# Pairing the stages of a linear-attention kernel across two batches, with paired loads and a new order

## The chip, the cores and the metric

The kernel runs on one core of a Trainium2 chip. A core has a matrix engine (TensorE, PE in the profile), a vector engine (VectorE, DVE), a scalar engine (ScalarE, ACT), a general engine (GpSimd, POOL) and a queue engine (SyncE, SP). Each runs its own instructions in order and waits on semaphores for the others. Sixteen DMA engines move data; DMAs are issued by SyncE, ScalarE and GpSimd, and in this kernel those from GpSimd convert float32 to bfloat16 on the way. The metric is the device time of one execution in microseconds (us).

## The reference

A recurrence with a decaying state per batch and head (4 batches, 8 heads, 768 steps, 48 features), followed by a two-layer network over all 3072 tokens (384 to 2048 to 384 features) with a leaky ReLU:

```python
for t in range(S):
    kt, vt, rt = k[:, :, t], v[:, :, t], r[:, :, t]
    cur = np.einsum('bhd,bhe->bhde', u[None] * kt, vt)
    y[:, :, t] = np.einsum('bhd,bhde->bhe', rt, state + cur)
    state = w[None, :, :, None] * state + np.einsum('bhd,bhe->bhde', kt, vt)
x = y.transpose(0, 2, 1, 3).reshape(B * S, H * D)
h = x @ w_in
g = np.maximum(0.01 * h, h)
out = g @ w_out
```

## The kernel before

**Stages.** The 768 steps of a batch are cut into 6 chunks of 128; a stage is one chunk of one batch, so there are 24. In the kernel before, stage n is chunk n % 6 of batch n // 6: all chunks of a batch come one after the other, and the state goes from stage n to stage n + 1, except at a batch's start.

**One stage.** Its steps have one letter each, followed by the stage's number:
- `k`, `r`, `v` load the stage's data with GpSimd (`load_one`, DMA on L284), 128 rows of 8 heads of 48 features. Stage 0 is loaded by SyncE and ScalarE instead (`load_early`, `v0` and the cast `U0`). Rings: 10 places for r and k side by side (`rk_sb`), 10 for v.
- `P` (`scaled`, L399) multiplies r and k by powers of the decay on VectorE. The result is transposed: stages 0 to 7 by TensorE (`T`, L421, with the ScalarE eviction `C`, L432), the rest by a DMA transpose that SyncE issues (`X`, L410).
- `A` (L481) forms the 128 x 128 scores of all 8 heads on TensorE, `M` masks them on VectorE: for stages 0 to 5 by a product (L491, L502, or `m` and `N`), for the others by a predicated copy (L505) into a tile whose diagonal is there already. That diagonal comes from `E`, `f`, `R` (VectorE, L442, L447, L452: u times k, times r, summed) and `L` (GpSimd, L467, which fills the tile). Stages 0 to 5 have `D` and `V` (VectorE) in their place.
- `K` (L539) is the product of keys and values on TensorE. `B` (`state_sum`, L570 or L573) adds the old state and `W` (`state_mul`, L578) decays the sum. Stages in `CARRY` add the old state on TensorE.
- `Y` (L609) adds scores times values and queries times state into PSUM; `O` (L627) evicts that to `xT` on ScalarE.

**The network.** It works on pairs m of stages 2m and 2m + 1. `J` (`up_two`, L664, 6 matmuls of 256 columns) is an eighth of the first layer, `j` (L673) its eviction with the leaky ReLU; stages 0 and 1 have some narrow ones (`G`, L642, 12 matmuls of 128 columns). The second layer is done in seven half-size products in place of eight (`Z`, L766, 8 matmuls of 192 columns each), with sums of `g` and of the weights on VectorE beforehand (`b`, L735; `t`, L716) and evictions `z` on ScalarE (L777, L782) and VectorE (L787). `o` stores a stage's 128 rows. `i` and `w` load the weights (L296, L300), `p` is the set-up of tables, masks and constants, `q` clears padding.

**Fills.** `F1.256.10@0` is one TensorE matmul on constants (L387) whose result nobody reads. There are 21, before and between the first transposes.

**The order.** `ORDER` is one list of steps, written out. `Sched.add` takes them in that order, and works out which semaphores each must wait for; each engine then plays its own steps in just that order. `@5` is the PSUM bank of a step (`@01` two of them); a step that writes a bank waits until the one before has been read. So a step that waits holds back all later steps of its engine, whatever they need.

## Time and profile before

| | |
|---|---|
| median of 3 runs | 164.97 us (164.47 to 165.57) |
| profiled execution | 165.07 us |
| its span, first to last instruction | 163.3 us |
| VectorE busy | 130.5 us, 260 instructions |
| ScalarE busy | 88.2 us, 194 instructions |
| GpSimd busy | 88.1 us, 101 instructions |
| data moved by DMA | 19.89 MB in 100234 packets |

The busy times are those of one profiled execution. A GpSimd DMA row shows the time in which GpSimd writes the transfer's descriptors; when its data have landed stands in rows of their own. Matmuls overlap each other, so the time of one is longer than the distance to the next. "L284" is a line of the kernel, "x23" a count, and a bracket behind a row of the time-ordered list tells how long the engine had been idle and what ended that.

### The profile page before, as it was taken

What the parts mean: (1) busy time and instruction counts of PE and PEld (TensorE: products, weight loads), DVE (VectorE), ACT (ScalarE), POOL (GpSimd) and SP (SyncE); (2) the same over time, 40 slices, a digit from 0 to 9 for tenths busy, and PEclk for the clock granted to TensorE, in tenths of its full rate; (3) what the DMA queues carried; (4) which work ended last, traced back from release to release, by engine and by line L of the source; (5) the groups of instructions that cost most, each with busy time, mean ns of one, the idle gap of its engine ahead of it and who ended that gap; (6) DMA issues with size and microseconds to landing.
All of it is one profiled execution on the core that took longest, in us unless ns stands there. A gap on an engine that the chain in (4) does not pass through costs nothing.

```text
span 163.3 us, 5367 instructions
## 1 busy us (share of the span) xinstructions
PE 154.8 (95%) x2299; PEld 137.6 (84%) x2299; DVE 130.5 (80%) x260; ACT 88.2 (54%) x194; POOL 88.1 (54%) x101
## 2 busy tenths in 40 slices
...
GB/s 105 137 167 167 154 174 163 186 204 144 145 121 161 100 151 152 130 145 87 150 131 211 264 128 151 230 4 0 62 199 52 0 4 0 0 18 180 4 98 193
DMA packets 100234, 19.89 MB, mean 122 GB/s; under 512 B 93169, under 2 KB 100210, under 8 KB 100210
## 3 DMA queue, kind: packets, MB, share of 16 engines
...
q10 hardware_dynamic: 1328, 0.39, 1.0%
...
## 4 chain that ended last, share of the span: by engine, by line
PE 60%; POOL 21%; DVE 9%; DMA 6%; issue 2%; POOLq 0%; DVEq 0%
PE ps_all L766 28%; PE ps_all L664 25%; POOL rk_sb L284 11%; DMA rk_sb<-in_r_dram 6%; POOL v_sb L284 4%; PE ps_all L609 3%; PE ps_all L481 2%; POOL w_out_sb L300 2%; POOL w_in_sb L296 2%; DVE qk L399 2%; DVE at L505 2%; POOL at L467 1%; PE ps_all L539 1%; DVE out_sb L787 1%; DVE s_tok L452 1%
## 5 line engine op out<-in xcount | busy, mean ns | idle before, releaser
L673 ACT ACTIVATE gT<-ps_all 128x512 bf16<-128x512 f32 x92 | 52.0, 604 | 29.3 <-PE ps_all L766 14.1
L664 PE MATMUL ps_all<-xT,w_in_sb 128*128 128x256 bf16 x552 | 66.6, 273 | 0.5 <-DVE at L505 0.5
L664 PEld LDWEIGHTS ps_all<-xT,w_in_sb 128*128 128x128 bf16 x552 | 52.4, 98 | 7.3 <-DVE at L505 0.8
L467 POOL TENSOR_SCALAR_AFFINE_SELECT at<-s_tok 128x1024 bf16<-128x1024 f32 x18 | 20.6, 1155 | 27.0 <-DVE s_tok L452 26.9
L766 PE MATMUL ps_all<-tw,gs 128*128 128x192 bf16 x288 | 28.3, 246 | 0.1
L735 DVE TENSOR_TENSOR gs<-gT 128x1024 bf16<-128x1024 bf16 x24 | 16.1, 686 | 11.1 <-ACT gT L673 5.8
L284 POOL DMA_DIRECT2D rk_sb<-in_k_dram x23 | 21.0, 918 | 7.2 <-DVE ku L442 6.4
L766 PEld LDWEIGHTS ps_all<-tw,gs 128*128 128x128 bf16 x288 | 24.0, 98 | 0.4 <-issue 0.3
L505 DVE CAST_PREDICATED at<-mask,ps_all 128x1024 bf16<-128x1024 uint16 x18 | 21.5, 1216 | 2.0 <-PE ps_all L481 1.8
L284 POOL DMA_DIRECT2D v_sb<-in_v_dram x23 | 21.1, 923 | 0.6 <-PE ps_all L539 0.6
L284 POOL DMA_DIRECT2D rk_sb<-in_r_dram x23 | 21.3, 932 | 0.0
L766 PE MATMUL ps_all<-w_out_sb,gT 128*128 128x192 bf16 x192 | 19.8, 246 | 0.0
L787 DVE TENSOR_TENSOR out_sb<-ps_all,snap 128x192 f32<-128x192 f32 x37 | 12.6, 351 | 5.9 <-PE ps_all L766 5.8
L627 ACT ACTIVATE xT<-ps_all 128x384 bf16<-128x384 f32 x24 | 11.0, 494 | 11.5 <-PE ps_all L609 10.3
L777 ACT ACTIVATE snap<-ps_all 128x192 f32<-128x192 f32 x36 | 11.1, 338 | 11.3 <-PE ps_all L766 10.3
L766 PEld LDWEIGHTS ps_all<-w_out_sb,gT 128*128 128x128 bf16 x192 | 16.1, 98 | 0.5
L399 DVE TENSOR_TENSOR qk<-rk_sb,tab 128x768 bf16<-128x768 bf16 x23 | 13.9, 611 | 2.9 <-DMA rk_sb<-in_r_dram 2.7
L609 PE MATMUL ps_all<-at,v_sb 128*32 128x128 bf16 x384 | 10.4, 220 | 1.1 <-DVE vs L560 1.1
L432 ACT ACTIVATE tp<-ps_all 128x512 bf16<-128x512 f32 x16 | 9.0, 596 | 3.9 <-PE ps_all L421 3.6
L609 PEld LDWEIGHTS ps_all<-at,v_sb 128*32 128x32 bf16 x384 | 8.0, 96 | 3.1 <-DVE vs L560 1.4
L766 PE MATMUL ps_all<-w_out_sb,gs 128*128 128x192 bf16 x96 | 9.9, 246 | 0.0
L782 ACT ACTIVATE out_sb<-ps_all 128x192 f32<-128x192 f32 x11 | 3.7, 332 | 11.3 <-PE ps_all L766 11.3
...
## 6 DMA issues: line engine op xcount, KB each, us to landing
...
w_out_sb<-in_moe_w_out_dram POOLq DMA_DIRECT2D x4, 384.0 KB, 11.1
tp<-qk SPq DMA_TRANSPOSE x16, 5.2
...
```

Of the source, the lines that this page charges most:

```text
L284: add("pool", lambda: G.dma_start(dst, src), W=[key], dma=f"{which}{n}")
L399: add("dve", lambda: V.tensor_tensor(qk[iq][:, :, 0:D], both, by, ALU.mult), R=[("r", n % NRK), ("k", n % NRK), "qtab", "ktab", ("qk0", iq ...
L467: add("pool", lambda: G.affine_select(out=at[ia][:, :, :, :].rearrange("p two m i -> p (two m) i"), in_=s_tok[i2][:, :].unsqueeze(2).to_br ...
L505: add("dve", lambda: V.copy_predicated(dst, mask[:, :].bitcast(mybir.dt.uint16).unsqueeze(1).to_broadcast([128, H, 128]), raw), R=keys + [ ...
L609: last = PE.matmul(ps_y[32 * q:32 * q + 32, 128 * s:128 * s + 128], a, m, start=first_mm and (s == 0 or whole), stop=last_mm and whole)
L627: add("act", lambda: A.activation(xT[m % NX][:, :, 128 * half:128 * half + 128], ps[i][:, 0:HD].rearrange("p (s t) -> p s t", t=128), AF.C ...
L664: last = PE.matmul(ps[i][:, 256 * f:256 * f + 256], w_in_sb[:, s, 128 * fb:128 * fb + 128], xT[ix][:, s, :], start=s == 0, stop=s == NSL - 1)
L673: add("act", lambda: A.activation(gT[ig][:, 2 * j:2 * j + 2, :].rearrange("p f t -> p (f t)"), ps[i][:, :], AF.Prelu, alpha=0.01), R=[key] ...
L735: add(eng, lambda: on.tensor_tensor(x[i][:, :, :], a, b, op), R=keys, W=[("gs", m % 2, i)])
L766: done = PE.matmul(ps[i][:, 0:NH], lhs[:, s, :], rhs[:, s, :], start=bool(opens) and s == 0, stop=s == HF - 1, skip_group_check=not (opens ...
L777: add("act", lambda: A.activation(snap[i2][j][:, :], ps[i][:, 0:NH], AF.Copy), R=[key], W=[("snap", i2, j)])
L787: add("dve", lambda: V.tensor_tensor(out_sb[io][:, cols], ps[i][:, 0:NH], snap[i2][j][:, :], ALU.add), R=[key, ("snap", i2, j), *after], W ...
```

## The change

- Stage n is now chunk n // 2 % 6 of batch n // 12 * 2 + n % 2. Stages 2m and 2m + 1 are the same chunk of two batches, and the state goes from stage n to stage n + 2. `CARRY` has stages 2 and 3 in place of 1 and 2 (and 0, which had no effect).
- From stage 2 on, `k`, `r` and `v` load both stages of a pair with one DMA each (`PAIRED`); the places of `rk_sb` are laid out so that the two stages lie side by side. `scaled` reads r and k of one stage from two stretches. v has 12 places in place of 10.
- Rows of the output are stored where the new numbering puts them.
- `ORDER` is new throughout and has no fills. GpSimd's list begins with the ramp, r1, k1, r2, k2, i0, v1, i1, v2, k4, r4, k6, r6; VectorE's, after the tables, with P0, P1, D0, P3, P2, M0. `INTER` is not used by the functions.

```diff
--- before.py
+++ after.py
@@ -22,57 +22,55 @@
 NSL = HD // 128
 
 VHW = {0}
-RINGS = (6, 8, 6, 6, 6, 3, 3, 8, 10, 10)
+RINGS = (6, 8, 6, 6, 6, 3, 3, 8, 10, 12)
 DIAG = {0, 1, 2, 3, 4, 5}
 SUMS_PE = set()
 KU_POOL = set()
 ST_POOL = set()
 GS_POOL = set()
-CARRY = {0, 1, 2}
+CARRY = {2, 3}
+INTER = 1
+PAIRED = {2, 4, 6, 8, 10, 12, 14, 16, 18, 20, 22}
 FIRST = {0}
 ORDER = """
-p3 p0 q1 k1 p10 p2 p8 p11 p4 F1.256.10@0 F1.256.2@1 k2 p5 p21@7 p6 p9 r1 p7 p15 p17 p13 p16 F1.512.18@6 v0 r2
-F1.128.8@5 p22 F1.256.1@6 q0 p14 p19 F1.128.28@0 p18 F1.128.18@1 q3 F1.256.9@2 q5 p23 F1.256.15@3 q4 i1 q2
-F1.256.12@4 p24 F1.128.24@5 F1.256.6@6 F1.256.0@7 r3 p31 P0.0 F1.512.1@0 P0.1 F1.256.17@1 T0.0@0 k3 F1.128.25@7
-F1.256.8@6 C0.0 F1.512.15@7 v1 P1 F1.128.9@1 T0.1@2 F1.512.8@3 P2 C0.1 T1.1@4 k5 p32 p27 U0 D0 A0@01 r5 p28
-T2.1@5 M0.1 T2.0@6 p30 F1.256.16@7 C2.1 T1.0@3 M0.0 K0@2 v2 p29 C1.0 V0 i0 C1.1 B0 Y0@7 C2.0 v3 A1@01 P3 A2@23
-m1.1 D1 r4 T3.1@4 O0 N1.1 T3.0@1 K1@5 M1.0 C3.0 k4 G0.1@6 V1 C3.1 B1 k7 Y1@7 D2 P5 r7 A3@01 O1 K2@4 D3 M3.0
-T5.1@5 i3 T5.0@7 V2 C5.0 G1.1@0 v4 M2 C5.1 G1.0@7 g1.1 k6 B2 g0.1 K3@5 G0.0@0 r6 V3 M3.1 Y2@6 g0.0 i2 P4 g1.0
-Y3@4 v7 O2 T4.1@7 O3 p1 A5@01 T4.0@6 M5.0 J1.0@2 v5 C4.0 P7 J1.2@0 C4.1 v6 D5 j1.0 B3 J1.1@6 m5.1 D4 w0 T7.0@7
...
-Z10.2 b11.2 Z10.3@7 z10.2 z11.0 Z11.1@0 z10.3 z9.4 Z10.4 Z9.5 z10.4 Z9.6 Z11.2@1 z9.6 z11.1 o19 Z11.3 z11.2 z9.5
-Z10.5 b11.3 o18 z11.3 Z11.4 z10.5 Z10.6 z11.4 z11.7 o23.0 Z11.5 z10.6 o20 o23.1 Z11.6@0 o21 z11.5 o22.1 z11.6
-o22.0
+p3 p0 p9 q1 p2 p14 p17 p8 r1 q2 p11 q0 p4 p18 p16 p5 k1 p10 p21@0 p6 p13 p15 r2 p7 v0 p22 k2 p24 p23 i0 P0.0
+P0.1 v1 T0.0@7 T0.1@6 P1 C0.0 i1 q3 T1.1@5 p19 p27 p31 p28 p32 p30 v2 p29 C0.1 C1.1 k4 D0 A0@67 U0 T1.0@0 K0@1
+r4 C1.0 P3 A1@23 P2 k6 T3.1@0 M0.0 T2.1@4 M0.1 T2.0@5 r6 V0 T3.0@6 C2.0 q4 Y0@7 D1 i3 m1.1 C2.1 N1.1 v4 B0 O0
+A2@34 M1.0 K1@5 C3.1 v6 C3.0 M2 G0.1@7 i2 V1 A3@01 p1 D3 Y1@6 B1 k8 D2 O1 q5 K2@2 M3.1 K3@3 w0 V2 G1.1@1 M3.0 w1
+Y2@4 w3 G1.0@0 P5 O2 w2 V3 T5.0@5 g1.0 T5.1@6 P4 r8 Y3@4 C5.0 B2 C5.1 G0.0@0 k10 O3 A5@56 g1.1 T4.1@2 T4.0@4 r12
+C4.1 P7 J1.0@1 M5.0 C4.0 J1.3@2 r10 m5.1 B3 T7.1@4 j1.3 D5 A4@56 P6 J1.1@3 g0.1 M4 T6.0@2 j1.1 J1.2@7 g0.0 N5.1
+T6.1@3 J0.6@5 D4 C6.0 b0.2 C6.1 K5@6 J1.7@0 C7.1 V5 K4@2 j1.0 B5 T7.0@3 V4 Y5@4 C7.0 Y4@6 O5 E6 J0.7@1 E7 O4 B4
+j1.7 J1.5@3 f7 j0.7 f6 J0.4@4 E9 j1.5 R7 A7@01 j0.4 W4 A6@23 L7 R6 J1.6@6 j1.2 W5 j0.6 J2.5@4 L6 M7 J0.5@7 k12
+J2.0@5 E8 j0.5 M6 J2.7@0 j1.6 k16 J1.4@1 j2.7 b0.0 K6@7 v12 j1.4 b1.2 Y7@6 Y6@0 b0.1 O7 J2.6@3 v8 O6 b1.0 J2.2@6
+j2.6 J3.3@2 j2.5 t0 J2.4@3 t2 J3.2@4 j2.4 J2.1@1 B6 f9 Z0.0@0 t1 Z1.0@3 j3.2 P8 Z0.1@7 j3.3 E10 f8 j2.0 K7@4 t3
+J2.3@2 z0.0 z1.0 j2.1 J3.7@5 W6 P9 j2.3 Z0.2 B7 X9 P11 J3.1@1 b1.1 Z1.1@2 j3.1 X8 P10 J3.0@4 z0.2 P12 j2.2
+Z0.3@1 b0.3 j3.0 P13 Z0.4 z0.1 z1.1 f10 X12 Z0.5 R9 W7 Z1.2 L9 E13 z0.4 Z1.3@6 R8 z1.2 E12 L8 J3.5@4 X10 z0.3
+z1.3 Z0.6 z0.5 b2.0 r14 J3.6@1 j3.5 f13 b1.3 X11 Z1.4 j3.7 r16 j3.6 A9@45 z1.4 A8@67 k18 Z2.0@1 M8 X13 Z1.5 k14
+M9 Z1.6 J3.4@6 k22 b2.1 Y8@7 R13 Y9@4 O8 b3.2 Z2.1@5 O9 b2.3 j3.4 K8@7 J4.4@4 z0.6 E11 z2.1 z1.5 z1.6 K9@6 R10
+J4.6@0 z2.0 f12 L10 J4.0@2 b3.0 j4.6 B8 J4.5@3 j4.0 B9 J4.7@0 r18 j4.5 f11 b3.1 J4.1@2 j4.4 R11 j4.7 A10@34 R12
+A11@67 j4.1 L11 Z2.2 M10 J4.3@0 v10 P17 J4.2@2 j4.3 M11 L12 Z2.3@3 j4.2 Z3.0@4 z2.2 v16 P16 P15 A12@67 z3.0
+Z3.1@0 M12 L13 Z3.2 z3.1 v14 b2.2 Z3.3@2 z3.2 E17 A13@67 z2.3 k20 b3.3 Z2.4 M13 K12@3 Z3.4 r20 Z2.5 z2.4 W9 v20
+Z3.5 B12 P18 Z4.0@6 v18 z3.4 Z2.6 W8 z3.5 b4.0 Y11@7 z2.6 Y10@3 P14 O11 Y12@0 f17 O10 X18 Y13@1 E16 Z3.6 O12 E15
+O13 K13@7 J5.7@3 X14 P19 J6.6@0 E14 j5.7 b4.2 J5.4@1 R17 J5.6@3 z2.5 j5.4 L17 f15 o0 J5.5@5 X16 j5.6 J6.4@1 z3.6
+b4.1 j5.5 J6.7@3 R15 j6.4 f16 J5.0@4 L15 X15 z3.3 j6.7 f14 J5.1@5 j6.6 E19 J6.5@1 R14 o1 J6.2@0 f19 j6.5 L14 X17
+B13 J6.0@2 b4.3 j6.2 r22 J6.3@3 j5.0 E18 j6.0 o4 J6.1@7 R19 X19 j6.3 f18 Z4.1@4 L19 j6.1 R18 z4.0 A15@01 A14@23
+L18 M15 J5.3@7 o7 Z4.2 j5.3 M14 Z4.3@0 z4.1 j5.1 K14@1 z4.2 J5.2@7 b6.0 E21 Z4.4 j5.2 B14 P20 Y14@5 Y15@7 z4.3
...
+z10.1 j11.7 J11.5@2 j11.6 Z11.0@1 j11.5 Z11.1@7 z10.0 b11.0 z9.6 Z10.2 z11.1 b11.1 z11.0 Z11.2@2 z9.5 z10.2
+b10.2 o18 Z10.3@5 o19 z11.2 o13 Z11.3 b11.3 Z11.4 z11.3 Z10.4 z11.4 z11.7 Z10.5 z10.4 o23.1 z10.3 Z10.6 z8.6
+z10.5 o17 Z11.5 z10.6 o21 Z11.6@0 z11.5 o23.0 o22.1 o20 z11.6 o22.0
 """
 
 
@@ -184,8 +182,8 @@
     HF, NH = NFB // 2, HD // 2
     w_in_sb = SB("w_in_sb", [128, NSL, DFF])
     w_out_sb = SB("w_out_sb", [128, NFB, HD])
-    rk_sb = SB("rk_sb", [128, NRK, 2, HD])
-    r_sb, k_sb = rk_sb[:, :, 0, :], rk_sb[:, :, 1, :]
+    rk_sb = SB("rk_sb", [128, NRK // 2, 2, 2, HD])
+    r_sb, k_sb = rk_sb[:, :, 0, :, :], rk_sb[:, :, 1, :, :]
     v_sb = SB("v_sb", [128, NV, H * E])
     w_row = SB("w_row", [1, HD], FP32)
     one_row = SB("one_row", [1, 128], FP32)
@@ -238,14 +236,24 @@
     def hd(x):
         return x.rearrange("p (h d) -> p h d", d=D)
 
+    def chunk(n):
+        return n // 2 % NC
+
+    def batch(n):
+        return n // (2 * NC) * 2 + n % 2
+
+    def rows_of(n):
+        at = S * batch(n) + L * chunk(n)
+        return slice(at, at + L)
+
     def early(which, n):
         return out_sb[4 + 2 * n + (which == "k")][:, :]
 
     def k_of(n):
-        return early("k", n) if n in FIRST else k_sb[:, n % NRK, :]
+        return early("k", n) if n in FIRST else k_sb[:, n % NRK // 2, n % 2, :]
 
     def r_of(n):
-        return early("r", n) if n in FIRST else r_sb[:, n % NRK, :]
+        return early("r", n) if n in FIRST else r_sb[:, n % NRK // 2, n % 2, :]
 
     def key_of(which, n):
         if n in FIRST:
@@ -263,25 +271,25 @@
 
 
     def load_early(which, n, eng):
-        src = {"k": k, "r": r}[which][0].rearrange("h t d -> t h d")[L * n:L * n + L, :, :]
+        src = {"k": k, "r": r}[which][batch(n)].rearrange("h t d -> t h d")[L * chunk(n):L * chunk(n) + L, :, :]
         dst, queue = early(which, n), {"act": A, "sp": SP}[eng]
         add(eng, lambda: queue.dma_start(dst.rearrange("p (h d) -> p h d", d=D), src),
             W=key_of(which, n), dma=f"{which}{n}")
 
     def load_one(which, n):
-        b, c = divmod(n, NC)
-        t0 = c * L
-        src = {"k": k, "r": r, "v": v}[which][b].rearrange("h t d -> t h d")[t0:t0 + L, :, :]
+        m, slots = (2 if n in PAIRED else 1), (NV if which == "v" else NRK)
+        i = n % slots
+        src = {"k": k, "r": r, "v": v}[which][batch(n):batch(n) + m].rearrange("b h t d -> t (b h) d")
+        src = src[L * chunk(n):L * chunk(n) + L, :, :]
         if which == "v":
-            dst = v_sb[:, n % NV, :].rearrange("p (h e) -> p h e", e=E)[:, :, 0:D]
+            dst = v_sb[:, i:i + m, :].rearrange("p b (h e) -> p (b h) e", e=E)[:, :, 0:D]
         else:
-            dst = {"k": k_sb, "r": r_sb}[which][:, n % NRK, :].rearrange("p (h d) -> p h d", d=D)
-        key = (which, n % (NV if which == "v" else NRK))
+            dst = {"k": k_sb, "r": r_sb}[which][:, i // 2, n % 2:n % 2 + m, :].rearrange("p b (h d) -> p (b h) d", d=D)
         if which == "v" and n in VHW:
             io = 6 + n
             add("sp", lambda: SP.dma_start(hd(out_sb[io][:, :]), src), W=[("o", io, 0), ("o", io, 1)], dma=f"v{n}")
         else:
-            add("pool", lambda: G.dma_start(dst, src), W=[key], dma=f"{which}{n}")
+            add("pool", lambda: G.dma_start(dst, src), W=[(which, i + j) for j in range(m)], dma=f"{which}{n}")
 
     def v_cast(n):
         io = 6 + n
@@ -394,9 +402,10 @@
     def scaled(n, half=None):
         iq = n % NQK
         if half is None:
-            both = rk_sb[:, n % NRK, :, :].rearrange("p w (h d) -> p (w h) d", d=D)
-            by = tab[:, :, :].rearrange("p w (h d) -> p (w h) d", d=D)
-            add("dve", lambda: V.tensor_tensor(qk[iq][:, :, 0:D], both, by, ALU.mult),
+            both = rk_sb[:, n % NRK // 2, :, n % 2, :].rearrange("p w (h d) -> p w h d", d=D)
+            by = tab[:, :, :].rearrange("p w (h d) -> p w h d", d=D)
+            to = qk[iq][:, :, 0:D].rearrange("p (w h) d -> p w h d", w=2)
+            add("dve", lambda: V.tensor_tensor(to, both, by, ALU.mult),
                 R=[("r", n % NRK), ("k", n % NRK), "qtab", "ktab", ("qk0", iq)], W=[("qp", iq), ("kp", iq)])
         elif half:
             add("dve", lambda: V.tensor_tensor(qk[iq][:, H:2 * H, 0:D], hd(k_of(n)), hd(ktab[:, :]), ALU.mult),
@@ -519,10 +528,10 @@
             R=["mask", ("at", ia, half)], W=[("at", ia, half)])
 
     def is_live(n):
-        return n % NC < NC - 1
+        return chunk(n) < NC - 1
 
     def is_carried(n):
-        return n in CARRY and n % NC > 0
+        return n in CARRY and chunk(n) > 0
 
     def keys_values(n):
         iq = n % NQK
@@ -566,17 +575,17 @@
         i, key = banks[("K", n)]
         kv = ps[i][:, 0:HD].rearrange("p (m e) -> p m e", e=2 * D)
         lock = [("kvlock", n)] if n in SUMS_PE else []
-        if n % NC == 0 or is_carried(n):
-            add("dve", lambda: V.tensor_tensor(st[(n + 1) % NT][:, :, :], kv, wl[:, :, :], ALU.mult),
-                R=[key, "wl0", "wl1"] + lock, W=[("st", (n + 1) % NT)])
+        if chunk(n) == 0 or is_carried(n):
+            add("dve", lambda: V.tensor_tensor(st[(n + 2) % NT][:, :, :], kv, wl[:, :, :], ALU.mult),
+                R=[key, "wl0", "wl1"] + lock, W=[("st", (n + 2) % NT)])
         else:
             add("dve", lambda: V.tensor_tensor(sum_t[n % 4][:, :, :], kv, st[n % NT][:, :, :], ALU.add),
                 R=[key, ("st", n % NT)] + lock, W=[("sum", n % 4)])
 
     def state_mul(n):
         eng, on = ("pool", G) if n in ST_POOL else ("dve", V)
-        add(eng, lambda: on.tensor_tensor(st[(n + 1) % NT][:, :, :], sum_t[n % 4][:, :, :], wl[:, :, :], ALU.mult),
-            R=[("sum", n % 4), "wl0", "wl1"], W=[("st", (n + 1) % NT)])
+        add(eng, lambda: on.tensor_tensor(st[(n + 2) % NT][:, :, :], sum_t[n % 4][:, :, :], wl[:, :, :], ALU.mult),
+            R=[("sum", n % 4), "wl0", "wl1"], W=[("st", (n + 2) % NT)])
 
     def outputs(n):
         it, ia, iv, is_ = n % NTP, n % NAT, n % NVS, n % NT
@@ -595,7 +604,7 @@
                 if kk > 0:
                     c1 = c0 + 16 + 32 * kk
                     one.append((v_sb[:, n % NV, c1:c1 + 32], at[ia][:, 1, p, :]))
-                if n % NC:
+                if chunk(n):
                     one.append((st[is_][:, p, 32 * kk:32 * kk + 32], tp[it][:, p, :]))
                 todo += [(s, a, m, i == 0, i == len(one) - 1) for i, (a, m) in enumerate(one)]
             return todo
@@ -617,7 +626,7 @@
         reads = [("v", n % NV), "v0", ("at", ia, 0), ("at", ia, 1), "ident", ("tp", it, 0)]
         if not whole:
             reads.append(("vs", iv))
-        if n % NC:
+        if chunk(n):
             reads.append(("st", is_))
         add("pe", emit, R=reads, W=[key])
 
@@ -696,12 +705,12 @@
     def stored(n, c=None):
         io = n % NO
         if c is None:
-            add("sp", lambda: SP.dma_start(out[128 * n:128 * n + 128, :], out_sb[io][:, :]),
+            add("sp", lambda: SP.dma_start(out[rows_of(n), :], out_sb[io][:, :]),
                 R=[("o", io, 0), ("o", io, 1)], W=[("out", n, 0)], dma=f"o{io}")
         else:
             cols = slice(NH * c, NH * c + NH)
             eng, queue = ("sp", SP) if c == 0 else ("act", A)
-            add(eng, lambda: queue.dma_start(out[128 * n:128 * n + 128, cols], out_sb[io][:, cols]),
+            add(eng, lambda: queue.dma_start(out[rows_of(n), cols], out_sb[io][:, cols]),
                 R=[("o", io, c)], W=[("out", n, c)], dma=f"o{io}{c}")
 
     def w_sum(i):
```

44 lines of the change are left out of this document (13 added, 31 removed).

## The prediction

> **What bounds the kernel now.** I read the busy shares first, then the chain in order of time, then the time-ordered list of TensorE with its idle notes.
>
> ```profile
> PE 154.8 (95%) x2299; PEld 137.6 (84%) x2299; DVE 130.5 (80%) x260; ACT 88.2 (54%) x194; POOL 88.1 (54%) x101
> ...
> 34.25 1.72 POOL rk_sb L284 x2
> 35.97 9.89 DMA rk_sb<-in_r_dram
> ...
> 62.62 2.14 PE ps_all L664 x18
> ...
> 148.75 11.89 PE ps_all L766 x144
> 160.64 0.02 issue
> 160.66 0.36 DVE out_sb L787
> ```
>
> The chain says GpSimd until 36 us, one r load until 45.9, VectorE until 62.6, then TensorE without a hole to 160.64. The first part misleads if read as "TensorE waits for loads until 62 us": a chain shows what ended last, not what TensorE did meanwhile. Its own list does (an idle time stands in brackets at a row's end):
>
> ```profile
> 16.85 0.33 PE L539 MATMUL ps_all<-v_sb,qk 128*128 128x96 bf16 x4
> ...
> 21.11 0.24 PE L609 MATMUL ps_all<-at,v_sb 128*32 128x128 bf16 x4
> ...
> 22.67 2.13 PE L664 MATMUL ps_all<-xT,w_in_sb 128*128 128x256 bf16 x18
> 24.64 0.39 PE L421 MATMUL ps_all<-ident,qk 128*128 128x128 bf16 x4
> ...
> 56.07 0.40 PE L481 MATMUL ps_all<-tp 48*128 48x128 bf16 x8 [1.39 <-DVE sum_t L573]
> ...
> 62.62 1.59 PE L664 MATMUL ps_all<-xT,w_in_sb 128*128 128x256 bf16 x13 [0.55 <-DVE at L505]
> ```
>
> From 16.85 us on it idles twice, 1.39 and 0.55 us, 1.94 in all. So the end is set by (a) when dense TensorE work starts, for which I take 22.67 us, the first wide up-projection J1.0; (b) the matmuls after it; (c) 1.94 us of stalls; (d) the tail behind 160.64. Only (a) and (c) can be won.
>
> What makes the 1.39 us stall stands in the list of all engines:
>
> ```profile
> 52.88 1.21 DVE L399 TENSOR_TENSOR qk<-rk_sb,tab 128x768 bf16<-128x768 bf16 x1
> ...
> 54.01 1.53 DVE L447 TENSOR_TENSOR ku<-rk_sb,ku 128x384 bf16<-128x384 bf16 x1
> 54.21 1.11 POOL L467 TENSOR_SCALAR_AFFINE_SELECT at<-s_tok 128x1024 bf16<-128x1024 f32 x1
> ...
> 55.94 0.34 DVE L787 TENSOR_TENSOR out_sb<-ps_all,snap 128x192 f32<-128x192 f32 x1
> 56.18 1.11 POOL L467 TENSOR_SCALAR_AFFINE_SELECT at<-s_tok 128x1024 bf16<-128x1024 f32 x1
> 56.20 2.34 DVE L505 CAST_PREDICATED at<-mask,ps_all 128x1024 bf16<-128x1024 uint16 x2
> ...
> L399 DVE TENSOR_TENSOR qk<-rk_sb,tab x23: 542/551/1209, 8.8 to 109.6; 128x768 bf16<-128x768 bf16 x23
> ...
> L447 DVE TENSOR_TENSOR ku<-rk_sb,ku x18: 345/351/1533, 30.9 to 112.3; 128x384 bf16<-128x384 bf16 x18
> ```
>
> Two VectorE products that take 0.55 and 0.35 us in the middle of their groups took 1.21 and 1.53 beside a GpSimd diagonal fill: 1.84 us lost. The eviction z1.3 (55.94) came after them, and the scores A8 of 56.07 write the bank that it empties.
>
> **The change, part by part.** The 21 fills go; the matmuls of the computation are the same in number (as many stages without a state, as many live ones, two carried ones as before). So (b) stays, and (d) too: the last steps are again z11.6 and o22.0 on the same queues.
>
> *Fewer, larger loads.*
>
> ```profile
> L284 POOL DMA_DIRECT2D v_sb<-in_v_dram x23 | 21.1, 923 | 0.6 <-PE ps_all L539 0.6
> L284 POOL DMA_DIRECT2D rk_sb<-in_k_dram x23 | 21.0, 918 | 7.2 <-DVE ku L442 6.4 <-POOLq L855 0.8
> L296 POOL DMA_DIRECT2D w_in_sb<-in_moe_w_in_dram x4 | 3.1, 786 | 0.0
> ```
>
> 69 issues become 36: three single ones and 33 pairs. A single is 128 rows times 8 heads, 1024 pieces, in 0.92 us; a w_in load is 128 times 3, 384 pieces, in 0.79. A pair, 2048 pieces, costs between 0.92 (pieces free) and 1.84 (twice a single); the line through the two rows gives 0.92 + 1024 x 0.13/640 = 1.13, which I take. GpSimd is then relieved of 66 x 0.92 - 33 x 1.13 = 23 us. None of it is TensorE time by itself: what counts is when data land, and those pieces are as many and as small as before.
>
> ```profile
> 1.31 1.93 POOL L284 DMA_DIRECT2D rk_sb<-in_k_dram  x2 [0.80 <-POOLq L855]
> ...
> 26.72 1.00 POOL L284 DMA_DIRECT2D rk_sb<-in_k_dram  x1
> ...
> 38.57 0.92 POOL L284 DMA_DIRECT2D rk_sb<-in_k_dram  x1
> DMA to landing us min/median/max: 4.4/4.4/4.4
> ...
> DMA to landing us min/median/max: 12.8/12.9/12.9
> ...
> DMA to landing us min/median/max: 9.9/10.9/11.3
> ```
>
> The three landing rows are for loads issued in 0 to 3, 24 to 28 and 36 to 40 us. The load of 26.72 landed about 39.6, that of 38.57 (twelfth, counting both) near 49.2: 9.6 us for 11 loads, 0.87 us each, with a backlog standing. That is the pace at which the DMA engines serve loads, hardly quicker than GpSimd issued singles. So pairing makes a load land no earlier, and the earlier member of a pair later.
>
> In the new order GpSimd does the ramp, r1, k1, then the pairs of r2 and k2. If r1 lands 4.4 us after an issue near 1.6, at 6.0, the k2 pair lands five loads later, 6.0 + 5 x 0.87 = 10.4; r4, twelve loads and two w_in loads (I allow 1.8 us each) behind r1, near 20.0.
>
> *The start on VectorE.* It runs in order, and the scaling of stages 3 and 2 (P3, P2) now stands ahead of the masking M0 of stage 0.
>
> ```profile
> 8.77 0.56 DVE L399 TENSOR_TENSOR qk<-rk_sb,tab 128x768 bf16<-128x768 bf16 x1 [2.15 <-DMA rk_sb<-in_r_dram]
> ...
> 10.61 1.28 DVE L491 TENSOR_TENSOR at<-ps_all,mask 128x512 bf16<-128x512 f32 x2
> ...
> 27.00 0.42 DVE L518 TENSOR_TENSOR at<-at,mask 128x512 bf16<-128x512 bf16 x1
> 27.34 0.55 DVE L560 TENSOR_TENSOR vs<-v_sb,ps_all 128x384 bf16<-128x384 bf16 x1
> 27.80 0.35 DVE L578 TENSOR_TENSOR st<-sum_t,wl 128x384 bf16<-128x384 bf16 x1
> ...
> 49.18 0.47 DVE qk L399
> ```
>
> From start to start an instruction takes 0.47 (P, V and B), 0.34 (D, N), 0.60 (half a mask) and 1.13 (a whole one, from the pair at 56.20). Up to what lets Y3 start, both orders hold the same VectorE work except B2, moved behind: 6 P, 4 V, 2 B = 5.6; 4 D, 1 N = 1.7; 5 half masks = 3.0; 1.1; small ones 0.6: 12.0 us. The tables are ready near 5.6, as now.
> - Waits before: 2.15 us for stage 1 at 8.77, and some tenths; Y3 ran at 21.11.
> - Waits after: stage 1 lands near 7, 0.5 us; D0 waits for the eviction C0.1, now behind four small ScalarE steps, 1.0 us; P3 for the k2 pair, from 9.3 to 10.4, 1.1 us; P5 for r4, about 0.5 us. Sum 3.1.
>
> V3 ends at 5.6 + 12.0 + 3.1 = 20.7 and Y3 starts there, 0.4 us earlier than before. Between Y3 and J1.0 there were 1.56 us (21.11 to 22.67); one narrow up-projection (G0.0) more is now there, 12 matmuls of 128 columns. The 18 of 256 columns at 22.67 took 1.97 us to the next row, 0.109 each, so 12 of half the width take 0.66. J1.0: 20.7 + 1.56 + 0.66 = 22.9, and with slower first transposes I take 23.1: **+0.4 us**. Shorter state chains (stage 1 no longer waits for stage 0, nor 3 for 2) don't show here, because VectorE's sum is the bound.
>
> *The middle.* By the same counting the masks of stages 8 and 9 have 0.5 us more VectorE work ahead than before, and the loads of 10 to 13 land as VectorE comes to them. But its products now meet the diagonal fills otherwise: of the four behind R9 and R8, in the order W7, E13, E12, f13, one starts with the fill and is held about 1 us, where two lost 1.84. I let the stalls fall from 1.94 to 0.6: **-1.3 us**. If E12 is held too, 1 us of it comes back.
>
> *Smaller edits.* The scaling reads its operand in two stretches of 384 instead of one of 768. Its output was already in stretches of 48, so I take nothing; if it lost its rate (768 results in 0.47 us; the mask's 1024 take 1.13), each would cost 0.85, 0.38 more, 5 us over the 13 ahead of stage 9. Twelve v places lengthen one memset by about 0.1 us, hidden by the wait for the tables. The rows of the output go elsewhere with the same pieces: nothing.
>
> *The fills.* They ran while TensorE had nothing else, so their time is free. What they may do for the matmuls after them shows in the first transposes:
>
> ```profile
> 6.52 0.63 PE L421 MATMUL ps_all<-ident,qk 128*128 128x128 bf16 x4
> ...
> 9.39 0.40 PE L421 MATMUL ps_all<-ident,qk 128*128 128x128 bf16 x4 [0.79 <-DVE qk L399]
> ...
> 0.00:10.00 10.00, 7.55 (x42) 4.25 (x42) 4.78 (x20) 5.01 (x10) 8.82 (x15) 1.00 1.36 134
> ```
>
> Four transposes took 0.63 us, later 0.40, though the granted clock reads 1.00 throughout: the first ones are slow. I put 0.2 us above for that.
>
> **Sum.** +0.4 - 1.3 = -0.9 us on the profiled execution (165.07: span 163.3 and 1.8 around it), 164.2. The median of the three runs, 164.97, lies 0.1 below it: **164.1 us**.
>
> **The rivals.**
> - *Loads land sooner* (0.27). GpSimd issues a pair at 0.57 us per load; if the engines follow at 0.7, k2 lands at 9.5, P3 waits 0.2 instead of 1.1, P5 not at all, and VectorE never waits in the middle: start -1.0, both stalls gone, -1.9. Time 164.97 - 2.9 = 162.1. For it: nothing shows what the engines do when issued faster. Against: 0.87 with a backlog. The Trainium skill, page "DMA: Bandwidth & Descriptors", section "Measured (HBM→SBUF, 128 partitions, SWDGE, issued from GpSimd)", gives about 0.67 us as the floor, that of 64 packets at 10.5 ns. A single load here puts 1024/16 = 64 pieces on each of 16 engines, so by that page k2 would land at 9.4 and this rival holds.
> - *Late pairs hold VectorE* (0.24), the one that ends slower. P3, P5, P7, the table t0 and P11, P12 each stand in order in front of masks and evictions, and each now waits for a whole pair. If a load takes 1.0 us, r4 lands 1.6 us later, and k12, some 30 loads behind r1, over 3 us later. VectorE passes it to TensorE: +2.2 over the median, 167.2. It decides from about 0.95 us per load. For it: between 40 and 48 us loads share the engines with transposes. Against: 0.87.
> - *TensorE stays slow without fills* (0.07). From T0 to J1.0 there are 12 groups of 4 transposes and 4 narrow projections of 12, at 0.055 each 5.3 us; scores, outputs and key-value groups I put at as much. If those 10.6 us all run at half speed, J1.0 comes near 6.5 + 21.2 = 27.7: +5, 170. Against it, matmuls at half speed fill the time better. The Trainium skill, page "TensorE: Matmul & The Clock Gate", section "Part 1: The HAM clock gate (the "warmup" mystery)", says that full speed comes after about 3.4 us of sustained work; the row agrees that the first are slow, and whether scattered work counts no run here shows.
> - *Nothing moves* (0.08). The state was not on the path, GpSimd's time neither; the same stalls at other places: 165.0.
>
> **How the numbers follow.** The forecast keeps 0.34, with its own range 162.9 to 165.9. One per cent, 1.65 us, is about what tells from no change here: faster means under 163.3, slower above 166.6. Faster: the first rival but for a few hundredths, and the forecast's lower edge, 0.30. Slower: second and third rival, 0.27. Within: 0.43. The range runs from 161.2 to 167.9, past the middles of the first two rivals, and leaves out the half-speed case and a lost scaling rate.
>
> **What would show it.** Pair issues near 1.13 us and landings at 0.87 per load; P3 idle for r or k until about 10.4; J1.0 near 23; one or two TensorE idles between 50 and 63 with under 1 us; then TensorE unbroken to the end. Wrong it would be by J1.0 outside 22 to 24, by a scaling over 0.6 us in the median, by holes in TensorE after 65 us, or by transposes still at 0.6 us beyond 12 us.

## The result, and the profile after

The changed kernel takes 169.54 us (median of 4 runs, 169.06 to 170.40), the kernel before on the same chip 165.27 (164.47 to 166.23): a ratio of 1.026, 95% interval 1.020 to 1.032. The change makes it slower by 4.3 us; 164.1 was forecast. (A ratio leaves out the executions over 1.5% above their kernel's fastest, medians and ranges hold all of them.) The profiled execution took 169.49 us, its span 167.4, which is 4.1 more than before.

Where the 4.1 us are shows in a table by stretches of the span: busy time of TensorE, with the number of its matmuls in brackets, weight loads, VectorE, ScalarE, GpSimd, granted clock, DMA share, GB/s. Before:

```profile
0.00:30.00 30.00, 26.26 (x414) 19.59 (x415) 22.39 (x57) 19.83 (x40) 28.82 (x39) 1.00 1.84 153
30.00:60.00 30.00, 28.61 (x442) 25.73 (x440) 28.01 (x52) 17.30 (x39) 21.54 (x24) 1.00 2.02 150
90.00:100.00 10.00, 10.00 (x164) 9.15 (x162) 9.82 (x21) 5.53 (x13) 4.15 (x5) 1.00 1.10 197
150.00:163.30 13.30, 10.63 (x129) 10.40 (x127) 5.63 (x15) 2.43 (x8) 0.00 (x0) 1.00 0.27 91
```

After:

```profile
0.00:30.00 30.00, 23.69 (x334) 18.06 (x335) 21.16 (x52) 17.67 (x36) 25.85 (x31) 1.00 1.91 155
30.00:60.00 30.00, 30.00 (x471) 27.14 (x472) 28.02 (x56) 17.57 (x37) 15.29 (x13) 1.00 1.91 161
90.00:100.00 10.00, 8.97 (x158) 8.06 (x156) 9.47 (x18) 5.38 (x11) 0.15 (x1) 1.00 1.00 153
150.00:167.40 17.40, 12.86 (x150) 12.27 (x147) 7.57 (x19) 4.82 (x13) 0.00 (x0) 0.99 0.36 125
```

By 30 us 334 matmuls are done where before it was 393 (414 less 21 fills): a late start. From 30 to 60 us TensorE has no hole, where before 1.39 us were open. From 90 to 100 us 1.03 us are new, and behind 150 us it idles 4.54 where it was 2.67.

Busy time hides slow matmuls, so I also kept a ledger: TensorE's steps in order, each with its steady start-to-start time (J and Z 0.66 us, A 0.28, T 0.22, Y about 0.5). They add up to 145.9 us in both kernels; what is lost up to a time is that time less the steps begun by then.

| TensorE's loss, us | before | after | difference |
|---|---|---|---|
| up to 30 us | 12.15 | 14.51 | +2.4 |
| 30 to 90 us | 2.40 | 0.68 | -1.7 |
| 90 to 150 us | 0.02 | 1.44 | +1.4 |
| 150 us to the last step Z11.6 | 0.00 | 1.72 | +1.7 |
| behind its start | 2.83 | 3.17 | +0.3 |

The start, VectorE's list (a bracket is idle time and what ended it):

```profile
9.07 0.43 DVE L445 TENSOR_TENSOR prod<-tp 128x512 bf16<-128x512 bf16 x1 [1.30 <-ACT tp L441]
10.50 1.03 DVE L408 TENSOR_TENSOR qk<-rk_sb,tab 128x768 bf16<-128x768 bf16 x2 [1.00 <-DMA rk_sb<-in_k_dram]
11.44 1.28 DVE L500 TENSOR_TENSOR at<-ps_all,mask 128x512 bf16<-128x512 f32 x2
...
20.41 0.55 DVE L408 TENSOR_TENSOR qk<-rk_sb,tab 128x768 bf16<-128x768 bf16 x1
20.88 0.55 DVE L569 TENSOR_TENSOR vs<-v_sb,ps_all 128x384 bf16<-128x384 bf16 x1
```

Second row: P3 and P2 wait for the k2 pair until 10.50, and the masks M0.0 and M0.1 (third row) stand behind them. Last row: V3, started at 20.88. TensorE's list, narrow up-projections of 12 equal matmuls:

```profile
15.55 1.48 PE L651 MATMUL ps_all<-xT,w_in_sb 128*128 128x128 bf16 x12
...
19.84 1.06 PE L651 MATMUL ps_all<-xT,w_in_sb 128*128 128x128 bf16 x12
...
21.52 0.83 PE L651 MATMUL ps_all<-xT,w_in_sb 128*128 128x128 bf16 x12
```

The same work takes 1.48, 1.06 and 0.83 us: TensorE is slow until about 20 us. The granted clock's column reads 1.00 there, but that is no reading: the trace's first record of the clock starts at 20.31 us (8.21 in the kernel before), and the column counts the time ahead of it as full speed. J1.0 starts at 24.97 (before: 22.67).

The later holes stand in the chain that ended last, and in TensorE's list:

```profile
88.16 0.55 SPq L708
88.71 0.04 issue
88.75 6.20 DMA tp<-qk
94.95 0.05 issue
95.00 0.40 PE ps_all L490 x8
...
158.00 3.81 DMA out_dram<-out_sb
161.81 0.02 issue
161.84 0.37 DVE out_sb L796
162.21 0.05 issue
162.25 2.17 PE ps_all L775 x24
```

```profile
95.00 0.40 PE L490 MATMUL ps_all<-tp 48*128 48x128 bf16 x8 [1.02 <-DMA tp<-qk]
...
162.25 0.83 PE L775 MATMUL ps_all<-tw,gT 128*128 128x192 bf16 x8 [1.54 <-DVE out_sb L796]
```

The scores A19 waited for the DMA transpose X19, issued at 88.75 and landed at 94.95. Z10.6 waited for a VectorE eviction of stage 21, and that for the store o13, issued at 158.00: stages 13 and 21 share place 5 of the output ring, and o13 stands behind o19 on SyncE.

### The profile page after: what moved, and what is told of

Its sections match the earlier page's. It is cut to its first block, busy times and chain, and to the rows that moved or that the text cites. A ratio compares the mean times of both kernels' runs of the same rounds, so it can differ in the third digit from the quotient of the medians.

```text
span 167.4 us, 5268 instructions
## 1 busy us (share of the span) xinstructions
PE 155.1 (93%) x2278; PEld 138.2 (83%) x2278; DVE 128.2 (77%) x260; ACT 89.0 (53%) x194; POOL 68.9 (41%) x68
## 4 chain that ended last, share of the span: by engine, by line
PE 75%; DVE 9%; DMA 7%; ACT 5%; issue 2%; SPq 1%; DVEq 0%; ACTq 0%
PE ps_all L673 28%; PE ps_all L775 27%; PE ps_all L618 5%; PE ps_all L490 5%; DMA tp<-qk 4%; PE ps_all L430 3%; DMA out_dram<-out_sb 2%; PE ps_all L548 2%; DVE gs L744 2%; PE ps_all L651 2%; DVE ku L456 2%; ACT tp L441 2%; DVE at L514 1%; DVE out_sb L796 1%; DVE s_tok L461 1%
## 5 line engine op out<-in xcount | busy, mean ns | idle before, releaser
L673 PE MATMUL ps_all<-xT,w_in_sb 128*128 128x256 bf16 x552 | 67.4, 273 | 0.3 <-DVE at L514 0.3
L476 POOL TENSOR_SCALAR_AFFINE_SELECT at<-s_tok 128x1024 bf16<-128x1024 f32 x18 | 21.4, 1198 | 51.7 <-DVE s_tok L461 48.0
L636 ACT ACTIVATE xT<-ps_all 128x384 bf16<-128x384 f32 x24 | 10.9, 492 | 16.4 <-PE ps_all L618 10.4
L775 PE MATMUL ps_all<-w_out_sb,gT 128*128 128x192 bf16 x192 | 19.1, 246 | 0.0
L292 POOL DMA_DIRECT2D v_sb<-in_v_dram x12 | 13.8, 1158 | 2.3 <-issue 2.3
L408 DVE TENSOR_TENSOR qk<-rk_sb,tab 128x768 bf16<-128x768 bf16 x23 | 13.1, 579 | 2.1 <-DMA rk_sb<-in_k_dram 1.0
L292 POOL DMA_DIRECT2D rk_sb<-in_r_dram x12 | 14.0, 1167 | 1.3 <-PE ps_all L430 1.0
L292 POOL DMA_DIRECT2D rk_sb<-in_k_dram x12 | 13.7, 1145 | 0.0
L490 PE MATMUL ps_all<-tp 48*128 48x128 bf16 x192 | 9.2, 232 | 2.9 <-ACT tp L441 1.7
L775 PE MATMUL ps_all<-tw,gT 128*128 128x192 bf16 x96 | 9.9, 246 | 1.5 <-DVE out_sb L796 1.5
L490 PEld LDWEIGHTS ps_all<-tp 48*128 48x128 bf16 x192 | 5.9, 99 | 5.8 <-ACT tp L441 2.5
```

The lines of the kernel that those rows point to most:

```text
L292: add("pool", lambda: G.dma_start(dst, src), W=[(which, i + j) for j in range(m)], dma=f"{which}{n}")
L408: add("dve", lambda: V.tensor_tensor(to, both, by, ALU.mult), R=[("r", n % NRK), ("k", n % NRK), "qtab", "ktab", ("qk0", iq)], W=[("qp", i ...
L476: add("pool", lambda: G.affine_select(out=at[ia][:, :, :, :].rearrange("p two m i -> p (two m) i"), in_=s_tok[i2][:, :].unsqueeze(2).to_br ...
L490: last = PE.matmul(ps[i][:, 128 * p:128 * p + 128], tp[it][at_rows, NP + p, :], tp[it][at_rows, p, :], start=True, stop=True)
L673: last = PE.matmul(ps[i][:, 256 * f:256 * f + 256], w_in_sb[:, s, 128 * fb:128 * fb + 128], xT[ix][:, s, :], start=s == 0, stop=s == NSL - 1)
L775: done = PE.matmul(ps[i][:, 0:NH], lhs[:, s, :], rhs[:, s, :], start=bool(opens) and s == 0, stop=s == HF - 1, skip_group_check=not (opens ...
```

## The experiments

All are the changed kernel with the edit shown, but for e2, which is the kernel before. "Loss" is that of the ledger; the kernel before on the same chips took 165.0 to 165.7 us.

| run | median, us | ratio to before (95%) | J1.0 at | loss to 30 us | loss from there to Z11.6 |
|---|---|---|---|---|---|
| before | 165.27 | 1 | 22.67 | 12.15 | 2.42 |
| changed | 169.54 | 1.026 (1.020 to 1.032) | 24.97 | 14.51 | 3.84 |
| e1_fills | 169.73 | 1.022 (1.018 to 1.026) | 24.13 | 13.77 | 3.80 |
| e2_before_nofills | 166.70 | 1.006 (1.004 to 1.009) | 24.05 | 13.54 | 2.20 |
| e3_o13 | 169.40 | 1.023 (1.019 to 1.028) | 24.18 | 13.82 | 3.72 |
| e4_x19 | 169.54 | 1.024 (1.019 to 1.029) | 24.21 | 13.85 | 3.96 |
| e5_o13 | 168.31 | 1.022 (1.014 to 1.030) | 24.29 | 13.93 | 5.06 |
| e6_singles | 172.29 | 1.043 (1.037 to 1.049) | 24.80 | 14.34 | 7.34 |
| e7_start | 172.32 | 1.040 (1.033 to 1.047) | 22.78 | 15.32 | 4.52 |
| e8_all | 168.09 | 1.017 (1.012 to 1.022) | 22.87 | 15.41 | 0.96 |
| e9_three | 166.52 | 1.008 (1.005 to 1.012) | 25.09 | not read | not read |
| e10_start | 168.53 | 1.020 (1.014 to 1.025) | 24.63 | 16.32 | 1.36 |
| e11_i1 | 172.85 | 1.048 (1.042 to 1.054) | 28.05 | 19.27 | 2.27 |
| e12_i0 | 167.30 | 1.009 (1.005 to 1.013) | 24.60 | 14.15 | 2.18 |
| e13_start | 166.24 | 1.000 (0.997 to 1.004) | 22.90 | 12.62 | not read |
| e14_r22 | 167.51 | 1.012 (1.008 to 1.017) | 22.73 | 12.71 | not read |
| e15_r14 | 168.50 | 1.017 (1.012 to 1.022) | 22.91 | 12.62 | 3.22 |

("Not read" stands where the profiled execution was one of the kernel's longest; the other figures of e9, e13 and e14, and those of e5, come from such an execution too.)

**The fills.** 16 of before's fills put back (and `p10`, the memset of their operand, moved forward); and, in e2, the 21 taken from the kernel before.

```diff
-... p21@0 p6 ... T1.1@5 p19
+... F1.256.10@1 F1.256.2@2 p21@0 F1.512.18@3 ... F1.256.0@1 p6 ... T1.1@5 F1.512.1@2 F1.512.15@3 F1.512.8@4 p19
```

> The changed kernel with 16 of the constant matmuls back: two before the matmul of the decay row, eleven behind it, three behind the first transposes of stage 1; the memset of their operand is moved forward. Theory (TensorE runs at half speed until 20.3 us because nothing keeps it busy before): the first transposes from 9 us on take 0.40 us for four instead of 0.61, J1.0 starts near 23.0 instead of 24.97, and the time falls by 1.9 us to about 167.6. Rival (VectorE's order and the pair loads set the start): the transposes get faster but J1.0 stays within 0.4 us of 24.97 and the time within 0.5 us of 169.5.

> The kernel before without its 21 constant matmuls, nothing else. Theory (half speed for want of work): TensorE turns fast only near 20 us, J1.0 starts 1.5 to 2.5 us later than 22.67, and the time rises by about 2 us to 167.2. Rival (fills are idle filler): J1.0 within 0.4 us of 22.67 and the time within 0.5 us of 165.3.

In the kernel before they are worth about 1.0 us (ratio 1.006), half of what the theory of e2 said. In the changed order J1.0 comes 0.84 earlier with them, where the theory of e1 said 2.0 and its rival 0.4 at most, and the time moves by less than the runs tell (1.026 to 1.022), as the rival said. Without fills the three later profiles e3, e4 and e5 had J1.0 at 24.2 to 24.3 too, because TensorE became quick earlier in them (their first clock records start at 14.2 to 15.1 us, e1's at 9.5); how early varies from execution to execution. So slow matmuls are at most 0.8 of the 2.3 us; the rest of the start is elsewhere. VectorE's list of e1 shows where:

```profile
20.73 0.56 DVE L408 TENSOR_TENSOR qk<-rk_sb,tab 128x768 bf16<-128x768 bf16 x1 [1.07 <-DMA rk_sb<-in_r_dram]
21.20 0.55 DVE L569 TENSOR_TENSOR vs<-v_sb,ps_all 128x384 bf16<-128x384 bf16 x1
```

With TensorE quick, P5 waits 1.07 us for the r4 pair, and V3 (second row), which needs no load, stands behind it.

**The stores.** o13 was moved forward twice, and three stores behind X19 once.

```diff
 e3_o13
-... o12 A23@12 ... z11.2 o13 Z11.3
+... o12 o13 A23@12 ... z11.2 Z11.3
 e4_x19
-... f15 o0 J5.5 ... R14 o1 J6.2 ... j6.0 o4 J6.1@7 R19 X19 j6.3
+... f15 J5.5 ... R14 J6.2 ... j6.0 J6.1@7 R19 X19 o0 o1 o4 j6.3
 e5_o13
-... z6.6 O22 ... z11.2 o13 Z11.3
+... z6.6 o13 O22 ... z11.2 Z11.3
```

> The changed kernel with the store of stage 13 moved on SyncE from behind the store of stage 19 to behind that of stage 12. Theory (the late store holds the place in which stage 21 is evicted, that eviction holds a PSUM bank, and TensorE waits 1.7 us at 160 to 162 us): the wait goes and the time falls by 1.6 us to about 167.9. Rival (the last evictions are late anyway): some other wait takes its place, and the time stays within 0.5 us of 169.5.

> The changed kernel with the stores of stages 0, 1 and 4 moved on SyncE behind the DMA transpose of stage 19. Theory (the transpose is issued at 88.75 us behind three stores of 2.2 us together, lands at 94.95, and the scores of stage 19 wait 1.1 us for it): it lands about 2 us earlier, the wait goes, and the time falls by about 1.1 us to 168.4. Rival (TensorE loses the same time later, at the masks or at the stores that are now later): the wait goes and the time stays within 0.4 us of 169.5.

> The changed kernel with the store o13 moved forward on SyncE, right behind z6.6, the last eviction into stage 13's rows. Theory (the store of stage 13 that stands behind o19 keeps place 5 of the output ring until 161.8 us, so the VectorE eviction of stage 21 and the matmuls Z10.6 wait): the TensorE idle of 1.71 us between Z10.5 and Z10.6 falls under 0.3, no wait appears before J9.5, and the time falls by 1.5 to 1.7 us to about 167.9. Rival (the last evictions and stores set the end whatever frees place 5): the idle moves to a later step, time 169.0 to 169.6.

In e3_o13 the store runs before two evictions of stage 13 (z6.4 and z6.6), so these parts of its rows are not in what is stored. The wait at Z10.6 went and an idle of 1.37 us came in front of Z6.6, for z6.4 must now let the store read first. e5_o13 stores behind both. TensorE's list there has no idle from 155 us to its end, and nothing new in front of J9.5. Three of its five times lie at 167.7 to 168.3, as the theory said; two, the profiled one among them, at 170.2, with this row:

```profile
95.66 0.40 PE L488 MATMUL ps_all<-tp 48*128 48x128 bf16 x8 [2.36 <-DMA tp<-qk]
```

A19 waited 2.36 us, though X19 was issued 1.5 us sooner than in the changed kernel (87.27). The idle cost more than its length, for the clock fell behind it (columns as in the tables of stretches above, the granted clock third from the end):

```profile
96.00:98.00 2.00, 2.00 (x21) 1.89 (x20) 1.63 (x4) 0.60 (x1) 0.00 (x0) 0.74 0.03 8
98.00:100.00 2.00, 2.00 (x12) 1.45 (x10) 1.73 (x2) 0.52 (x1) 0.00 (x0) 0.50 0.91 199
```

The clock's record has 0.50 from 96.97 us on for 3.41 us, in which half speed loses 1.7. With 1.3 us more idle than in the changed kernel that is 3.0 us, all that the ledger has more in this execution (5.06, against 3.84 less the 1.72 of the tail). The mean granted clock of the two long executions is 0.99, that of the three short ones 0.997 to 1.00; only one of the five has a trace. In e4_x19 X19 was issued at 85.85, A19 did not wait, and the place of its wait was taken at once:

```profile
94.38 0.36 DVE L794 TENSOR_TENSOR out_sb<-ps_all,snap 128x192 f32<-128x192 f32 x1 [1.10 <-DMA out_dram<-out_sb]
```

The eviction z4.3 waited for o0; TensorE idled 0.55 us behind it, and 1.90 in front of Z10.6. So the tail's cause is shown (1.72 us in the ledger, 0.04 in e5_o13); that the stores ahead of X19 make it late is not.

**The loads.** Each pair as two singles.

```diff
-PAIRED = {2, 4, 6, 8, 10, 12, 14, 16, 18, 20, 22}
+PAIRED = set()
-... r2 p7 v0 p22 k2 p24 ...
+... r2 r3 p7 v0 p22 k2 k3 p24 ...
```

> The changed kernel with every pair of loads split into two single loads, one behind the other at the place of the pair; state, order of the other engines and v places as in the changed kernel. Theory (the DMA engines are the pace, so pairing wins and loses little): r4 lands about one load, 0.9 us, earlier, GpSimd is busy about 22 us more, J1.0 stays within 0.8 us of 24.97, time 169.0 to 170.5. Rival (pairs hold the start, because P5 waits for both halves of r4): J1.0 near 24.0, time near 168.6. Third (the saved GpSimd time is what the new order needs): diagonal fills come late, TensorE idles over 2 us more between 50 and 100 us, time over 171.

The third case held: 172.29. The start hardly moves (J1.0 24.80), and 3.5 us more are lost behind 30 us. VectorE's and GpSimd's lists:

```profile
34.78 2.87 DVE L586 TENSOR_TENSOR st<-sum_t,wl 128x384 bf16<-128x384 bf16 x1
37.57 1.21 DVE L513 CAST_PREDICATED at<-mask,ps_all 128x1024 bf16<-128x1024 uint16 x1
```

```profile
35.08 2.35 POOL L475 TENSOR_SCALAR_AFFINE_SELECT at<-s_tok 128x1024 bf16<-128x1024 f32 x2
```

The singles push two diagonal fills to where a 0.35 us product of VectorE runs; it takes 2.87, and TensorE waits 1.28 for the mask behind it. It waits another 0.97 for VectorE at 74.67, and 1.9 in front of scores at 91.47 and 98.41 (1.0 in the changed kernel). Nor do the single loads land sooner: r4 at 19.54 and r5 at 20.30, the pair at 19.53 in the changed kernel. The paired loads are a gain of about 2.7 us in this order, not a cost: the loss is the order's.

**The start.** Three reorderings, on top of fills.

```diff
 e7_start (as e1_fills)
-... V2 G1.1@1 ... P5 O2 w2 V3 T5.0@5 g1.0 T5.1@6 P4 r8 Y3@4 C5.0 B2 C5.1 G0.0@0 k10 O3 A5@56 g1.1 T4.1 T4.0 ... J1.0
+... V2 G1.1@1 ... O2 w2 V3 g1.0 r8 Y3@4 B2 G0.0@0 O3 g1.1 J1.0@1 P5 T5.0@5 P4 T5.1@6 C5.0 C5.1 k10 A5@56 T4.1 T4.0 ...
 e10_start (as e9_three below; also V3 to T4.0 as in e7_start, but A5 behind T4.1 and T4.0)
-... P3 A1@23 P2 T3.1 M0.0 T2.1 M0.1 T2.0 V0 T3.0 C2.0 Y0@7 D1 m1.1 ... M2 G0.1 V1
+... A1@23 M0.0 M0.1 V0 Y0@7 P3 P2 T3.1 T2.1 T2.0 T3.0 C2.0 D1 m1.1 ... V1 M2 G0.1
 e11_i1 (as e10_start)
-... C0.0 i1 q3 ... r4 C1.0
+... C0.0 q3 ... r4 i1 C1.0
```

> The changed kernel with its 16 fills of before's kind (as in e1_fills) and another order at the start: V3 ahead of P5 and P4 on VectorE; on TensorE Y3, G0.0 and the first wide up-projection J1.0 ahead of the transposes of stage 5. Theory (P5 in front of V3 waits for the pair of r4, landing near 20.7 us, and that holds Y3 at 21.90): V3 runs at 19.6, Y3 near 20.3, J1.0 near 21.9 in place of 24.13, and the time falls by 1.0 to 1.6 us below e1_fills, to about 168.4. Rival (what waits for r4 is needed at once by what follows): TensorE idles the same 1 to 1.5 us behind J1.0, in front of the transposes of stage 5 or the scores A5, time 169.3 to 169.8.

> As e9_three, with another order at the start: on VectorE M0.0, M0.1 and V0 ahead of P3 and P2, V1 ahead of M2, V3 and B2 ahead of P5 and P4; on TensorE Y0 ahead of the transposes of stages 3 and 2, and Y3, G0.0, J1.0 and the transposes of stage 5 and 4 in this order, ahead of the scores A5. Theory (the start is late because VectorE stands idle for the pairs of k2 and r4 in front of masks that have their data): Y0 near 11.4 us, Y1 near 14.6, Y3 near 19.2, J1.0 near 20.6, and TensorE's loss up to 30 us falls from 13.8 to 12.1 us, the figure of the kernel before; time 1.5 us below e9_three, 164.9 or less, at or below the kernel before. Rival (the landing of r4 alone sets it): Y3 is early, the loss up to 30 us stays over 13.3, time within 0.6 us of e9_three.

> As e10_start, with the weight load i1 behind the r4 pair on GpSimd in place of ahead of v2 and k4. Theory (r4 lands when its turn in the DMA queue comes): r4 lands about 1.8 us sooner, near 19, P5 no longer waits, and the time falls another 0.3 to 1.0 us. Rival (VectorE has no free time there, so nothing is won, or J1.3 then waits for i1): within 0.3 us of e10_start.

All three missed, by waits of their own making. e7_start has J1.0 at 22.78, as early as the kernel before, and loses 1.6 us more up to 30 us than e1_fills: A5 waits 0.95 for the evictions of stage 5, J1.3 another 0.47. When dense work starts says little if the work behind it is not ready. In e10_start Y0 runs at 11.90, but TensorE idles 1.44 us in front of the scores of 15.13, for evictions of ScalarE, and m1.1 stands behind C2.0 there, so that VectorE waits for it:

```profile
14.62 0.43 DVE L527 TENSOR_TENSOR at<-at,mask 128x512 bf16<-128x512 bf16 x1 [1.41 <-ACT at L521]
```

In e11_i1 the narrow projection G0.1 needs i1 (TensorE's list):

```profile
19.50 1.46 PE L651 MATMUL ps_all<-xT,w_in_sb 128*128 128x128 bf16 x12 [4.09 <-DMA w_in_sb<-in_moe_w_in_dram]
```

In both the clock falls too: 0.50 from 16.60 us on for 3.41 us in e10_start, from 17.24 on for 6.83 us in e11_i1. So their J1.0, at 24.63 and 28.05, is late by half speed as well as by the waits, and they don't price the order alone.

**Put together.** e8_all is e7_start with o13 as in e5_o13 and the stores o1 and o4 behind X19; e9_three the same without e7's start.

> The order of e7_start, o13 as in e5_o13, and the two stores o1 and o4 moved behind the transpose X19 while o0 stays. Theory (each is a separate stall): the gains add, 169.7 less 1.3 less 1.6 less 0.9, about 165.9, level with the kernel before. Rival (the stalls cover a shared lag of VectorE or of the output ring): they overlap, 167 or more.

> The changed kernel with the 16 fills, o13 right behind z6.6 and the stores o1 and o4 behind the transpose X19; the order at the start otherwise as in the changed kernel. Against the two that it is made of it lacks the start of e7_start. Theory (the slow clock, the store in front of X19 and the store of stage 13 each cost what their idle shows, and a reordered start only moved the wait for r4): TensorE loses 13.8 us up to 30 us, where e8_all lost 15.4, and nothing over 0.5 at X19 and Z10.6; time 1.5 us below e8_all, 166.5. Rival (DMA transposes wait again, or the output ring catches up): 167.5 or more.

e8_all is 1.040 - 1.017 = 0.023, 3.8 us, below e7_start (3.5 between the two profiled executions): the two store edits remove the late holes (0.96 us lost behind 30 us, where e7_start lost 4.52). Its 168.09 is over the 165.9 of its theory all the same. e9_three came out at the forecast 166.5, but not by the forecast's account: its profiled execution (168.07, its longest) has J1.0 at 25.09, for there the r4 pair landed only at 21.57, and A19 waits 0.90 for X19. Fills and stores bring the ratio from 1.026 to 1.008, and 1.3 us remain, most of them at the start. Two kernels ask what they are:

```diff
 e12_i0 (as e9_three)
-... p23 i0 P0.0 ... r4 C1.0 ... Y2@4 w3 G1.0@0 P5 ... g1.0 T5.1@6 ... Y3@4 C5.0 B2 C5.1 G0.0@0 k10 O3 A5@56 g1.1 T4.1 T4.0
+... p23 P0.0 ... r4 i0 C1.0 ... Y2@4 w3 P5 ... T5.1@6 C5.0 C5.1 ... Y3@4 B2 G1.0@0 O3 g1.0 A5@56 T4.1 T4.0 G0.0@0 g1.1
 e13_start (as e12_i0)
-... P3 A1@23 P2 T3.1 M0.0 T2.1 M0.1 T2.0 V0 T3.0 C2.0 Y0@7 D1 m1.1 C2.1 N1.1 B0 O0 A2@34 M1.0 K1@5 ... M2 G0.1 V1 ... D2
+... A1@23 M0.0 M0.1 V0 Y0@7 m1.1 P2 P3 T2.1 T2.0 T3.1 T3.0 C2.0 C2.1 O0 D1 K1@5 N1.1 B0 M1.0 A2@34 V1 ... M2 D2 G0.1
```

> As e9_three, with the weight load i0 behind the r4 pair on GpSimd, and G1.0 and G0.0, the two narrow projections that read it before J1.0, moved behind Y3 on TensorE (A5 and the transposes of stages 5 and 4 between them). Theory (the rest of the start's loss is the landing of the r4 pair, which comes when its turn in the DMA queue comes): r4 lands 1.5 to 1.8 us sooner, near 19, P5 runs without a wait, Y3 starts near 20.8, TensorE's loss up to 30 us falls from 13.8 to 13.1 or less, and the time by 0.5 to 1.0 us to about 165.7. Rival (VectorE's own order is the bound up to Y3, and r4 was just in time): the loss stays within 0.3 of 13.8, time within 0.4 us of 166.5.

> As e12_i0, and the masks of stage 0 with V0 ahead of the scaling P2 and P3 on VectorE, V1 ahead of M2, D2 right behind M2; on ScalarE the copy m1.1 ahead of the evictions C2.0 and C2.1; on TensorE Y0 ahead of the transposes of stages 2 and 3, and K1 ahead of A2 (e10_start had m1.1 behind C2.0 and A2 ahead of K1, and waited for that). Theory (VectorE idles for the k2 pair in front of masks that have their data): Y0 near 11.6 us, Y1 near 15.3, Y3 near 20, TensorE's loss up to 30 us another 0.5 to 0.9 less than e12_i0, time 165.0 to 165.3, level with the kernel before. Rival (stages 2 and 3 come later by what stages 0 and 1 gain): within 0.4 us of e12_i0, or slower.

In e12_i0 the r4 pair lands at 17.08, early enough: P5 runs at 19.68 without a wait. But V3 still ends only at 20.6, Y3 starts at 21.03 (21.90 in e1_fills), and TensorE halts once inside it:

```profile
21.70 0.23 PE L618 MATMUL ps_all<-at,v_sb 128*32 128x128 bf16 x2 [0.44 <-issue]
```

("issue" is a halt for which the profile shows no wait.) The time does not move, and the rival held: VectorE's own order is the bound up to Y3. In e13_start the start came out as its theory says; VectorE's list:

```profile
9.81 1.29 DVE L500 TENSOR_TENSOR at<-ps_all,mask 128x512 bf16<-128x512 f32 x2 [0.24 <-PE ps_all L490]
11.02 0.55 DVE L569 TENSOR_TENSOR vs<-v_sb,ps_all 128x384 bf16<-128x384 bf16 x1
11.48 1.02 DVE L408 TENSOR_TENSOR qk<-rk_sb,tab 128x768 bf16<-128x768 bf16 x2
...
18.71 0.55 DVE L408 TENSOR_TENSOR qk<-rk_sb,tab 128x768 bf16<-128x768 bf16 x1
19.17 0.55 DVE L569 TENSOR_TENSOR vs<-v_sb,ps_all 128x384 bf16<-128x384 bf16 x1
```

VectorE does the masks of stage 0 (first row) while the k2 pair lands. No wait for a pair is left up to V3, which (last row) runs at 19.17 in place of 20.88, and the loss up to 30 us falls to 12.62. The ratio is 1.000, but it counts eight of twelve executions; all twelve lie between 164.33 and 168.79, with the median at 166.24, 0.9 us above that of the kernel before. The profiled one, 166.97, loses part of the gain again: TensorE idles 1.26 us in front of A12 at 68.67, since P17 waits 1.00 us for the r16 pair. So the paired kernel with the order mended is level with the kernel before in its better executions, and never clearly faster.

**What delays X19.** The last two move loads, on top of e13_start.

```diff
 e14_r22
-... v20 ... v18 z3.4 ... j6.2 r22 J6.3@3
+... v20 ... v18 r22 z3.4 ... j6.2 J6.3@3
 e15_r14 (as e14_r22)
-... W7 Z1.2 L9 E13 ... b2.0 r14 J3.6 ... j3.7 r16 j3.6
+... W7 Z1.2 r14 r16 L9 E13 ... b2.0 J3.6 ... j3.7 j3.6
```

> As e13_start, with the load of the r22 pair issued right behind v18, near 76 us, in place of near 86.5, between the diagonal fills. Theory (X19 lands late because the pieces of the r22 pair share the DMA engines with it, not because of the stores in front of it): X19 lands within 4.5 us of its issue, where the runs so far took 5.2 to 8.3, the scores A19 never wait, and the time falls by 0.3 to 1.0 us, to 165.2 to 165.9. Rival (another transfer delays X19): it takes 5 us or more, and the time stays within 0.4 us of 166.2.

> As e14_r22, with the loads of the r14 and r16 pairs ahead of the diagonal fills L9 and L8 on GpSimd, which is idle from 42 to 49 us. Theory (the start won by e13_start is given back where P17 waits 1.0 us for the r16 pair at 66 us): P17 no longer waits and TensorE's 1.4 us in front of A12 at 68 us fall under 0.5; time 0.7 to 1.2 us below e14_r22. Rival (the loads collide with the transposes X9 to X13, issued from 46 us on): A9 and A8 wait 1 us or more at 52 to 55 us, and the time stays level or rises.

Both are slower than e13_start. In e14_r22 X19 takes 5.25 us, so its rival held. In e15_r14 TensorE no longer idles in front of A12, as its theory says, and A19 no longer waits, but X19 still takes 4.95 us, and other scores now wait for earlier transposes (the first row is A8, as its rival said):

```profile
55.38 0.40 PE L490 MATMUL ps_all<-tp 48*128 48x128 bf16 x8 [0.95 <-DMA tp<-qk]
...
88.94 0.62 PE L490 MATMUL ps_all<-tp 48*128 48x128 bf16 x16 [1.25 <-DMA tp<-qk]
```

A load moved away from one transpose falls on another: X14 took 6.3 us in e13_start, 9.0 in e14_r22 and 8.9 in e15_r14. What delays X19 in the changed kernel is in part open. It is not that stores stand ahead of it: with o1 and o4 behind, in e8, e9, e12 and e13, it takes 6.2 to 7.8 us. The r22 pair is the cause at most in part: from 86 to 96 us the queue of the GpSimd loads has 2064 packets in the changed kernel and 18 in e15_r14, and X19 goes from 6.20 to 4.95 only, where X22 takes 3.1.

## Why the prediction was wrong

The forecast was 0.9 us less, and the span grew by 4.1. Of these 5.0 us the ledger puts 2.0 at the start and 3.4 behind 90 us; the middle came out 0.4 better. So two steps failed, and the later one was the larger.

- **The start, +0.4 us, measured +2.3: the first step that failed.** Three terms of it held: the k2 pair frees P3 at 10.50 (10.4 forecast), the r4 pair lands at 19.53, or 20.61 in e1_fills ("near 20.0"), and from Y3 to J1.0 it is 2.24 us (1.56 + 0.66 = 2.22). Wrong was "V3 ends at 20.7 and Y3 starts there". With fills V3 ends at 21.67: 0.3 us more waiting than the 3.1 counted (1.30 for C0.1, 1.01 for k2, 1.07 for r4), and 0.6 more work and short pauses than the 12.0. In the profiled execution without fills V3 ends at 21.34, but Y3 starts only at 22.73: TensorE, which was taken to have time to spare up to Y3, is then itself late, with Y2 at 20.84 and narrow projections of 1.48 and 1.06 us. The 0.2 us put in for that were 0.8 there, and near 0.1 in e3, e4 and e5.
- **The waits at the start belong to the order.** The 1.1 us for P3 and 0.5 for P5 stood in the working, and rightly. But M0, behind P3, had its data: in e13_start it runs at 9.81, ahead of the k2 pair. e12_i0 against e13_start (loss to 30 us 14.15 to 12.62, medians 167.30 to 166.24) shows the order of a few VectorE, ScalarE and TensorE steps to be worth 1.1 to 1.5 us.
- **The middle, -1.3 us, held:** 30 to 90 us lose 0.7 us in place of 2.4. A8 and A9 do not wait; the products beside the fills of 50.77 and 52.55 take 0.34 to 0.36 us, so not even the one counted on was held. The second rival, late pairs holding VectorE, has its waits at the start (1.0 us at P3, 1.1 at P5 with fills) but not its cause, loads of 0.95 us or more; in the middle TensorE waits for no pair.
- **"TensorE unbroken to the end", with the tail (d) unchanged: the second step that failed, +3.4 us in the ledger.** It put nothing there. The forecast checked only that the last steps are z11.6 and o22.0, and not each store's place on SyncE against the place of the output ring that it frees, nor each transpose's issue against its reader. o13 behind o19 cost 1.5 us of idle, gone in e5_o13, and A19's wait for X19 1.0 us in the profiled execution.
- **Pairs.** Issue 1.16 us (1.13 forecast):

```profile
L292 POOL DMA_DIRECT2D rk_sb<-in_r_dram x12 | 14.0, 1167 | 1.3 <-PE ps_all L430 1.0
L408 DVE TENSOR_TENSOR qk<-rk_sb,tab 128x768 bf16<-128x768 bf16 x23 | 13.1, 579 | 2.1 <-DMA rk_sb<-in_k_dram 1.0
```

  The scaling in two stretches keeps its rate (0.58 us on the mean), and 0.87 us per load held: r1 landed at 5.62 and r4, twelve loads and two weight loads of 1.9 later, at 19.53, which is 0.85. By the estimate from the Trainium skill, page "DMA: Bandwidth & Descriptors", section "Measured (HBM→SBUF, 128 partitions, SWDGE, issued from GpSimd)", which gives about 0.67 us as a floor, P3 would have waited until 9.4; 10.50 was measured, and the loads here lie above that floor on the mean. But "none of it is TensorE time by itself" is wrong of the relief of GpSimd: in this order it is worth about 2.7 us (e6_singles).
- **The slow-TensorE rival** put 5 us on the start for the fills that go; at J1.0 it is 0.1 to 0.8 in the changed order and 1.4 in the one before (24.05 in e2, 22.67 with fills). The Trainium skill, page "TensorE: Matmul & The Clock Gate", section "Part 1: The HAM clock gate (the "warmup" mystery)", asks for about 3.4 us of sustained work; the rows of 15.55, 19.84 and 21.52 agree that the scattered work ahead of them, from 9 us to past 15, didn't bring the full speed. In e3, e4 and e5 the same work did, at 14.2 to 15.1 us.
